# A fused attention and two-stage expert kernel: partial sums of the first stage added by GpSimd's transfers, with other priorities

## The chip, the cores and the metric

The program runs on one core of one Trainium2 chip. The metric is the device time of one execution in microseconds. Three executions of the kernel before gave 853.74, 858.54 and 864.12 us, so the time before is their median, 858.54 us.

## The reference

Three layers follow each other on 2304 tokens of width 512 (4 batches x 576 tokens, 8 heads of 64):

```python
# attention in a causal window of 64 keys
scores = where(0 <= rel < 64, q @ k.T / 8, -1e9);  x = softmax(scores) @ v
# first moe stage: dense, d_ff 2048; w_in and w_out are float64
h = x @ w_in;  g = h - tanh(h);  x = g @ w_out
# second moe stage: top 1 of 8 experts, d_ff 1024
logits = (x / |x|) @ (emb / |emb|).T / tau
e = argmax(logits);  gate = softmax(logits)[e]
out = gate * (relu(x @ w1[e]) @ w2[e])
```

## The kernel before

Tokens are cut into 9 chunks `c` of 256. The program has two parts. In the first, up to some 561 us of the profiled execution, come the attention (`t_attn`, 18 units `n`, two per chunk, four heads each), the decoding of the float64 weights (`t_decode`, 32 halves), the first moe stage (`t_moe1`, 72 steps) and the routing of each finished chunk (`t_route`). In the second the experts follow one after another. The change lies in the first part.

**A step.** `t_moe1` takes two blocks of 128 of the d_ff columns for one chunk. TensorE makes `h` (`mm1`, 24 matmuls of 128x256 on the lines of `mm3`), ScalarE and VectorE make `g - tanh` and split it in a high and a low part `gh` (VectorE lines L639, L648, L652, L656, L666), and TensorE multiplies by `w_out` into two PSUM accumulators `o` (`mm2`, 12 matmuls of 128x512).

**Segments.** While weights are still being decoded, chunks 0 to 3 are worked on in four segments of two steps each, so that every decoded block serves four chunks at once. The list `order` says which segment comes when; chunks 4 to 8 then run their eight steps in one segment. At a segment's end `t_sum` takes the sums out of PSUM. The first segment of a chunk is copied to a buffer of the pool `st` (4 buffers of 128x1024) and stored to `partd[c]` in DRAM. Each later one first loads `partd[c]` to an `st` buffer, VectorE adds the two accumulators to it (L698), and it is stored again, except after the last segment: there the sum `x2` goes on to `t_route`. That stores it, takes its squares on ScalarE (L726), a power on GpSimd (L735), transposes it on TensorE (L751), makes logits and slots, and scatters 8-byte entries of a list with GpSimd (L848, two scatters per chunk, each waiting for the one before).

The `st` buffers also hold raw weights, chunks of `x` on their way from DRAM, and the transposed `x2` of the routing.

**The order of the work.** Nothing is ordered by hand. Every function calls `SC.add` with the engines that can do a task, a duration for each, what it reads, writes and allocates, and a priority. `Sched.run` then plays the program in its own time and gives an idle engine the ready task of the lowest priority; an engine's queue afterwards runs in exactly that order. So a changed priority or duration reorders every engine. A GpSimd transfer is planned with 1.04 for its issue and `lat` on top, and a hand-over between engines with `OTHER = 0.21`. The priorities come from `slot_t` (TC per block while weights are decoded, TM after that), `TA` (how far apart attention units are), `AHEAD` and `WLEAD`:

```python
T0, TC, TM = 8, 3.7, 2.9
TA = 14
AHEAD, LEAD, WLEAD = 10, 12.0, 6.0
```

Of the kernel before, what the change touches and what calls it, by code (L numbers as in the profile page):

```python
# [16 lines left out]
ALU = mybir.AluOpType  # L17
# [144 lines left out]
def attn_moe_moe2(ctx, tc, q, k, v, w_in, w_out, emb, tau, w1, w2, out):  # L162
# [58 lines left out]
    def copies(o, i, act, dve):  # L221
        return {ACT: (act, lambda: nc.scalar.copy(out=o(), in_=i())), DVE: (dve, lambda: nc.vector.tensor_copy(out=o(), in_=i()))}  # L222
# [116 lines left out]
    def t_decode(f, o, w, pr):  # L339
        raw, tmp = Buf("st"), Buf("tmp")  # L340

        def load():
            r = raw.t.bitcast(U32)
            if o == 0:
                nc.sync.dma_start(
                    out=r.rearrange("p (k f) -> p k f", k=KD),
                    in_=w_in.bitcast(U32)[:, f * 256:(f + 1) * 256].rearrange("(k p) f -> p k f", p=P),
                )
            else:
                nc.sync.dma_start(out=r, in_=w_out.bitcast(U32)[f * P:(f + 1) * P, :])  # L350

        def words(i):
            return raw.t.bitcast(U32).rearrange("p (n w) -> p n w", w=2)[:, :, i]

        hi = lambda: w.t[:, o * 512:o * 512 + 512]
        lo = lambda: w.t[:, 1024 + o * 512:1536 + o * 512]
        ti = lambda: tmp.t.bitcast(U32)
        tf = lambda: words(1).bitcast(F32)

        def d1():  # L360
            nc.scalar.activation(out=tmp.t, in_=words(1).bitcast(F32), func=AF.Abs)

        def d2():
            nc.vector.tensor_scalar(out=tmp.t, in0=tmp.t, scalar1=float(2.0 ** -15), scalar2=None, op0=ALU.max)

        def d3():
            nc.vector.tensor_scalar(
                out=ti(), in0=ti(), scalar1=3, scalar2=0x3FFFFFF8,
                op0=ALU.logical_shift_left, op1=ALU.bitwise_and,
            )  # L370

        def d4():
            nc.vector.scalar_tensor_tensor(
                out=ti(), in0=words(0), scalar=29, in1=ti(), op0=ALU.logical_shift_right, op1=ALU.bitwise_or
            )

        def d5():
            nc.vector.scalar_tensor_tensor(
                out=words(1), in0=words(1), scalar=0xC0000000, in1=ti(), op0=ALU.bitwise_and, op1=ALU.bitwise_or
            )  # L380

        SC.add({DMA: (1.5, load)}, writes=[(raw, 0)], allocs=[raw], prio=pr - 6.0)
        SC.add(
            {ACT: (0.52, d1)}, reads=[(raw, 0)], writes=[(tmp, 0)], allocs=[tmp] + ([w] if o == 0 else []), prio=pr
        )
        SC.add({DVE: (0.335, d2)}, writes=[(tmp, 0)], prio=pr)
        SC.add({DVE: (0.335, d3)}, writes=[(tmp, 0)], prio=pr)
        SC.add({DVE: (0.6, d4)}, reads=[(raw, 0)], writes=[(tmp, 0)], prio=pr)
        SC.add({DVE: (0.6, d5)}, reads=[(tmp, 0)], writes=[(raw, 0)], prio=pr)
        SC.add({ACT: copies(hi, tf, 0.52, 0.335)[ACT]}, reads=[(raw, 0)], writes=[(w, o)], prio=pr)  # L390

        def sub(eng):
            return lambda: eng.tensor_tensor(out=lo(), in0=tf(), in1=hi().bitcast(F32), op=ALU.subtract)  # L393

        SC.add({DVE: (0.6, sub(nc.vector))}, reads=[(raw, 0), (w, o)], writes=[(w, 2 + o)], prio=pr)
# [7 lines left out]
    def t_attn(n, pr, direct, spill):  # L403
# [52 lines left out]
        def s_mm():  # L456
# [7 lines left out]
                        )  # L464

        SC.add(
            {PE: (1.1, s_mm)}, reads=lq, writes=[(as_[0], 0), (as_[1], 0)], allocs=[*as_, pr_], prio=pr + 1.5
        )
        st = {}

        def mx(hh):
            if hh == 0:
                st["m"] = small("mx", [P, 2 * NB], bufs=3)
            for i in range(NB):
                first = [(c * NB + 2 * (i % 2) + d) % (S // BLK) == 0 for d in range(2)]
                m_ = 1 + hh if first[0] else 2 - hh if first[1] else 0
                nc.vector.tensor_tensor_reduce(
                    out=pr_.t[:, hh * NB + i, :], in0=as_[hh].t[:, i * P:(i + 1) * P], in1=mask[m_],
                    scale=-SCALE, scalar=3.0e38, op0=ALU.add, op1=ALU.min, accum_out=st["m"][:, hh * NB + i:hh * NB + i + 1],
                )  # L480

        def ex(hh):
            if hh == 0:
                st["den"] = small("den", [P, 2 * NB], bufs=3)
            for i in range(hh * NB, (hh + 1) * NB):
                nc.scalar.activation(  # L486
                    out=pr_.t[:, i, :], in_=pr_.t[:, i, :], func=AF.Exp, bias=st["m"][:, i:i + 1], scale=-1.0,
                    accum_out=st["den"][:, i:i + 1],
                )
# [20 lines left out]
                nc.tensor.transpose(out=ap[hh].t[:, i * P:(i + 1) * P], in_=pr_.t[:, hh * NB + i, :], identity=ident)  # L510

        for hh in range(2):
            SC.add({DVE: (0.9, lambda hh=hh: mx(hh))}, reads=[(as_[hh], 0)], writes=[(pr_, hh)], prio=pr + 1.5)
        for hh in range(2):
            SC.add({ACT: (1.54, lambda hh=hh: ex(hh))}, writes=[(pr_, hh)], prio=pr + 1.5)
        SC.add({DVE: (0.29, dn)}, writes=[(pr_, 0), (pr_, 1)], prio=pr + 1.5)
        for hh in range(2):
            SC.add(
                {DVE: (0.6, lambda hh=hh: nm(hh)), ACT: (1.2, lambda hh=hh: nm_act(hh))}, writes=[(pr_, hh)], prio=pr + 1.5
            )  # L520
            SC.add(
                {PE: (0.43, lambda hh=hh: tp(hh))}, reads=[(pr_, hh)], writes=[(ap[hh], 0)], allocs=[ap[hh], pT[hh]],
                prio=pr + 3,
            )
            SC.add(
                copies(lambda hh=hh: pT[hh].t, lambda hh=hh: ap[hh].t, 0.48, 0.6), reads=[(ap[hh], 0)],
                writes=[(pT[hh], 0)], prio=pr + 3,
            )
# [75 lines left out]
    def t_moe1(c, f, acc, first, last, pr):  # L604
# [74 lines left out]
        for j in range(2):  # L679
            SC.add(  # L680
                {PE: (1.39, lambda j=j: mm2(j))}, reads=[(wt[f + j], 1), (wt[f + j], 3), (gs, 0), (gs, 1)],
                writes=[(acc[0], 0), (acc[1], 0), ("mm2", c, f + j)], prio=pr + 3.0,
            )


    def t_sum(c, acc, more, last, near, pr):

        x2 = Buf("st")
        if more:
            SC.add(  # L690
                {DMA: (1.5, lambda: nc.sync.dma_start(out=x2.t, in_=partd[c]))},
                reads=[("part", c), ("mm2", c, near)], writes=[(x2, 0), (x2, 1)], allocs=[x2], prio=pr - 12.0,
            )
        for i in range(2):
            h = slice(i * DM, (i + 1) * DM)
            alts = copies(lambda h=h: x2.t[:, h], lambda i=i: acc[i].t, 0.48, 0.6)
            if more:
                alts = {DVE: (0.6, lambda i=i, h=h: nc.vector.tensor_tensor(  # L698
                    out=x2.t[:, h], in0=acc[i].t, in1=x2.t[:, h], op=ALU.add))}
            SC.add(alts, reads=[(acc[i], 0)], writes=[(x2, i)], allocs=[x2] if i == 0 and not more else [], prio=pr)  # L700
        if not last:
            SC.add(
                {DMA: (1.5, lambda: nc.sync.dma_start(out=partd[c], in_=x2.t))},
                reads=[(x2, 0), (x2, 1)], writes=[("part", c)], prio=pr + 2.0,
            )
        return x2
# [518 lines left out]
    setup2()  # L1225
    t_setup()
    SC.free[POOL] = 5.5
    T0, TC, TM = 8, 3.7, 2.9
    TA = 14

    def slot_t(s):
        return T0 + TC * min(s, KF) + TM * max(s - KF, 0)
# [3 lines left out]
    order += [(1, 4, 8, ""), (0, 4, 8, ""), (0, 8, 12, ""), (1, 8, 12, ""), (3, 8, 12, "load"), (2, 8, 12, "load")]  # L1236
    order += [(2, 12, KF, ""), (3, 12, KF, ""), (1, 12, KF, "load"), (0, 12, KF, "load")]
    order += [(c, 0, KF, "load") for c in range(4, NC)]
    AHEAD, LEAD, WLEAD = 10, 12.0, 6.0
    start, due, s_ = {}, {}, 0  # L1240
    for c, f0, f1, how in order:
        start[c, f0] = s_
        for f in range(f0, f1):
            due.setdefault(f, slot_t(s_ + f - f0))
        s_ += f1 - f0
    t_weights(lambda f, o: due[f] - WLEAD + 3.0 * o)
    for n in range(NC * NU):
        c = n // NU
        first = [x[3] for x in order if x[0] == c]
        t_attn(  # L1250
            n, min(TA * n, slot_t(start[c, 0]) - AHEAD + 5.0 * (n % NU)) if c else 1.0 * n,
            first[0] if first[0] != "load" else None, "load" in first,
        )
    for c, f0, f1, how in order:
        if how == "load":
            t_xload(c, slot_t(start[c, f0]) - LEAD)
        acc = [Buf("o") for _ in range(2)]
        s_ = start[c, f0]
        for f in range(f0, f1, 2):
            t_moe1(c, f, acc, f0, f1 - 1, slot_t(s_ + f - f0))  # L1260
        end = slot_t(s_ + f1 - f0)
        x2 = t_sum(c, acc, f0 > 0, f1 == KF, f1 - 5 if f1 - 5 > f0 else f0, end - 12.0 if c + 1 < NC else 0.0)
        if f1 == KF:
            t_route(c, x2, end if c + 1 < NC else 0.0)
        if c == NC - 2:
            t_turns(end)
            t_list(0, 0, end)
# [180 lines left out]
```

## Time and profile before

| | |
|---|---|
| time, median of three | 858.54 us (853.74 to 864.12) |
| the profiled execution | 861.28 us, span 859.5 us |
| mean granted TensorE clock | 0.971 |
| TensorE busy | 788.2 us, 92% of the span |
| VectorE busy | 604.9 us, 70% |
| ScalarE busy | 483.3 us, 56% |
| GpSimd busy | 89.8 us, 10% |
| DMA | 111.39 MB, of it 13.13 MB on GpSimd's queue |

The shares are means over two parts with different limits. In the slices of the page VectorE stands at 9 tenths up to about 300 us and at 6 or 7 after that, while TensorE is at 7 to 9 in the first third and at 9 behind it. Busy time of TensorE counts a matmul to its modelled end, which reaches over the next one's start, so the distance between starts is the better price of a matmul; the same holds for VectorE's short latencies.

### The profile page before, as it was taken

To read this page: it belongs to the slowest core of one execution; us is meant where nothing else is said; L and a number is where in the kernel's file an instruction comes from. 1 tells how busy PE (TensorE), PEld (TensorE's weight loads), DVE (VectorE), ACT (ScalarE), POOL (GpSimd) and SP (SyncE) were. 2 spreads that over 40 slices of the span, in tenths; PEclk is the share of its full clock that TensorE was granted. 3 is DMA by queue.
4 is the path that set the end of the run, shared out by engine and by line. 5 is a ranking of instruction groups with operands and counts; after the bars stand their busy time and mean duration, and the time that the engine had idled before them with its cause. 6 is when DMAs were issued, how large, how long until landed. Compare 5 with 4: busy or idle time off the path is not lost. (4 is left out here: it accounts for less than half of the span.)

```text
span 859.5 us, 15577 instructions
## 1 busy us (share of the span) xinstructions
PE 788.2 (92%) x5703; PEld 687.3 (80%) x5703; DVE 604.9 (70%) x1498; ACT 483.3 (56%) x1121; POOL 89.8 (10%) x116
## 2 busy tenths in 40 slices
PE   4788799999899899999899999896999998997995
PEld 4577687988798789898788988775889887886984
DVE  6999999999999677767557678972177377244720
ACT  5799788867695658555555566731244343233421
POOL 2000000000002110010101001012022122121210
PEclk9899999999999999999999999997999999998998
DMA  9765754657654621100100004535067376235511
GB/s 288 239 205 153 240 175 151 201 176 239 204 168 88 155 73 38 62 1 1 50 1 25 1 26 144 183 116 171 13 195 239 108 241 225 75 100 174 161 40 37
DMA packets 67436, 111.39 MB, mean 130 GB/s; under 512 B 8580, under 2 KB 44420, under 8 KB 67344
## 3 DMA queue, kind: packets, MB, share of 16 engines
q1 hardware_dynamic: 62448, 97.07, 35.7%
q0 software_dynamic: 4896, 13.13, 4.9%
q8 instruction: 53, 0.87, 0.5%
q14 instruction: 39, 0.32, 0.1%
HBM read 89.57 MB, written 21.66 MB: 129 GB/s over the span
## 5 line engine op out<-in xcount | busy, mean ns | idle before, releaser
L600 PE MATMUL h<-x,w 128*128 128x256 f32 x712 | 206.6, 290 | 10.0 <-DVE g L652 9.4
L601 PE MATMUL h<-x,w 128*128 128x256 f32 x712 | 203.5, 286 | 2.0 <-DVE x L576 1.9
L602 PE MATMUL h<-x,w 128*128 128x256 f32 x712 | 203.0, 285 | 0.3 <-DVE w L393 0.2
L600 PE MATMUL o<-w,gh 128*128 128x512 f32 x464 | 188.7, 407 | 6.3 <-ACT gh L662 5.9
L602 PE MATMUL o<-w,gh 128*128 128x512 f32 x464 | 184.9, 399 | 3.6 <-DVE gh L666 2.2
L601 PE MATMUL o<-w,gh 128*128 128x512 f32 x464 | 184.0, 397 | 0.0
L600 PEld LDWEIGHTS h<-x,w 128*128 128x128 f32 x712 | 137.8, 194 | 17.6 <-issue 9.7
L601 PEld LDWEIGHTS h<-x,w 128*128 128x128 f32 x712 | 138.0, 194 | 6.1 <-DVE x L576 2.7
L602 PEld LDWEIGHTS h<-x,w 128*128 128x128 f32 x712 | 137.8, 194 | 0.8 <-DVE w L393 0.8
L602 PEld LDWEIGHTS o<-w,gh 128*128 128x128 f32 x464 | 88.4, 190 | 29.8 <-DVE gh L666 6.4
L600 PEld LDWEIGHTS o<-w,gh 128*128 128x128 f32 x464 | 88.6, 191 | 25.4 <-ACT gh L662 6.6
L601 PEld LDWEIGHTS o<-w,gh 128*128 128x128 f32 x464 | 88.9, 192 | 14.1
L222 ACT CAST w<-st 128x512 fp32r<-128x512 f32 x116 | 70.2, 629 | 33.1 <-DMA st<-in_moe_w_dram 21.4
L866 DVE TENSOR_TENSOR w<-st,w 128x512 fp32r<-128x512 f32 x128 | 82.8, 686 | 4.3 <-ACT w L222 3.3
L639 DVE SCALAR_TENSOR_TENSOR g<-g 128x512 f32<-128x512 f32 x72 | 49.5, 688 | 30.6 <-ACT g L631 30.4
L644 ACT ACTIVATE g<-h 128x512 f32<-128x512 f32 x72 | 42.9, 596 | 38.2 <-DVE g L648 31.6
L627 ACT ACTIVATE g<-h 128x512 f32<-128x512 f32 x72 | 42.6, 594 | 36.9 <-PE h L602 31.6
L662 ACT CAST gh<-g 128x512 fp32r<-128x512 f32 x72 | 44.1, 616 | 33.6 <-DVE g L656 29.4
L652 DVE TENSOR_TENSOR g<-h,g 128x512 f32<-128x512 f32 x72 | 49.4, 687 | 17.4 <-ACT g L644 16.2
L978 ACT ACTIVATE gh<-h 128x256 fp32r<-128x256 f32 x50 | 19.1, 383 | 73.3 <-PE h L602 54.8
L648 DVE TENSOR_TENSOR g<-h,g 128x512 f32<-128x512 f32 x72 | 49.6, 689 | 8.8 <-ACT g L644 5.2
L486 ACT ACTIVATE pr<-pr,mx 128x128 f32<-128x128 f32 x144 | 55.7, 391 | 0.1
(179 smaller groups left out, 1292.4 us busy)
## 6 DMA issues: line engine op xcount, KB each, us to landing
st<-in_moe_w_dram SPq DMA_DIRECT2D x64, 512.0 KB, 5.3
st<-in_moe_w_in_dram SPq DMA_DIRECT2D x16, 512.0 KB, 4.3
st<-in_moe_w_out_dram SPq DMA_DIRECT2D x16, 512.0 KB, 4.7
v<-in_v_dram SPq DMA_DIRECT2D x16, 512.0 KB, 3.7
part<-st SPq DMA_DIRECT2D x12, 512.0 KB, 2.7
st<-part SPq DMA_DIRECT2D x12, 512.0 KB, 9.6
k<-in_k_dram SPq DMA_DIRECT2D x16, 320.0 KB, 5.3
q<-in_q_dram SPq DMA_DIRECT2D x18, 256.0 KB, 3.0
```

The source lines that it names most:

```text
L222: return {ACT: (act, lambda: nc.scalar.copy(out=o(), in_=i())), DVE: (dve, lambda: nc.vector.tensor_copy(out=o(), in_=i()))}
L486: nc.scalar.activation(out=pr_.t[:, i, :], in_=pr_.t[:, i, :], func=AF.Exp, bias=st["m"][:, i:i + 1], scale=-1.0, accum_out=st["den"][:, i ...
L600: nc.tensor.matmul(out=ps, lhsT=ah, rhs=bh, start=start, stop=False)
L601: nc.tensor.matmul(out=ps, lhsT=ah, rhs=bl, start=False, stop=False)
L602: nc.tensor.matmul(out=ps, lhsT=al, rhs=bh, start=False, stop=stop)
L627: {ACT: (0.48, lambda: nc.scalar.activation(out=u(), in_=hp.t, func=AF.Square))},
L639: {DVE: (0.6, lambda: nc.vector.scalar_tensor_tensor(out=sq(), in0=sq(), scalar=SQ_B, in1=u(), op0=ALU.add, op1=ALU.mult))},
L644: {ACT: (0.48, lambda: nc.scalar.activation(out=u(), in_=hp.t, func=AF.Tanh))},
L648: {DVE: (0.6, lambda: nc.vector.tensor_tensor(out=sq(), in0=hp.t, in1=sq(), op=ALU.mult))},
L652: {DVE: (0.6, lambda: nc.vector.tensor_tensor(out=u(), in0=hp.t, in1=u(), op=ALU.subtract))},
L662: {ACT: (0.52, lambda: nc.scalar.copy(out=gh(), in_=sq()))}, reads=[(g, 1), (acc[0], "-"), (acc[1], "-")],
L866: return lambda: eng.tensor_tensor(out=w.t[:, b], in0=raw.t[:, a], in1=w.t[:, a].bitcast(F32), op=ALU.subtract)
```

## The change

`t_sum` no longer loads the partial sum. Every segment's accumulators are copied to an `st` buffer, by ScalarE or VectorE, whichever the scheduler finds free. The first segment is stored as before. A middle segment is added to `partd[c]` in DRAM by a transfer that GpSimd issues. The last segment's copy is the destination of such a transfer: `partd[c]` is added to the rows of `x2` in SBUF, and everything in `t_route` waits for that. Both are planned with `lat=3.0`. The priorities of weight loads, score matmuls, attention units, `mm2` and `t_sum` change too.

```diff
-        SC.add({DMA: (1.5, load)}, writes=[(raw, 0)], allocs=[raw], prio=pr - 6.0)
+        SC.add({DMA: (1.5, load)}, writes=[(raw, 0)], allocs=[raw], prio=pr - 8)
...
-                writes=[(acc[0], 0), (acc[1], 0), ("mm2", c, f + j)], prio=pr + 3.0,
+                writes=[(acc[0], 0), (acc[1], 0), ("mm2", c, f + j)], prio=pr + 2,
...
-        if more:
-            SC.add(
-                {DMA: (1.5, lambda: nc.sync.dma_start(out=x2.t, in_=partd[c]))},
-                reads=[("part", c), ("mm2", c, near)], writes=[(x2, 0), (x2, 1)], allocs=[x2], prio=pr - 12.0,
-            )
         for i in range(2):
             h = slice(i * DM, (i + 1) * DM)
-            alts = copies(lambda h=h: x2.t[:, h], lambda i=i: acc[i].t, 0.48, 0.6)
-            if more:
-                alts = {DVE: (0.6, lambda i=i, h=h: nc.vector.tensor_tensor(
-                    out=x2.t[:, h], in0=acc[i].t, in1=x2.t[:, h], op=ALU.add))}
-            SC.add(alts, reads=[(acc[i], 0)], writes=[(x2, i)], allocs=[x2] if i == 0 and not more else [], prio=pr)
-        if not last:
+            SC.add(
+                copies(lambda h=h: x2.t[:, h], lambda i=i: acc[i].t, 0.48, 0.6), reads=[(acc[i], 0)], writes=[(x2, i)],
+                allocs=[x2] if i == 0 else [], prio=pr,
+            )
+        if last and not more:
+            return x2
+        if last:
+            SC.add(
+                {POOL: (1.04, lambda: nc.gpsimd.dma_start(out=x2.t, in_=partd[c], accum_op=ALU.add))},
+                reads=[("part", c)], writes=[(x2, 0), (x2, 1)], prio=pr + 1.0, lat=3.0,
+            )
+        elif more:
+            SC.add(
+                {POOL: (1.04, lambda: nc.gpsimd.dma_start(out=partd[c], in_=x2.t, accum_op=ALU.add))},
+                reads=[(x2, 0), (x2, 1)], writes=[("part", c)], prio=pr + 2.0, lat=3.0,
+            )
+        else:
...
-    T0, TC, TM = 8, 3.7, 2.9
-    TA = 14
+    T0, TC, TM = 8, 4.3, 2.9
+    TA = 20
...
-    AHEAD, LEAD, WLEAD = 10, 12.0, 6.0
+    AHEAD, LEAD, WLEAD = 12, 12.0, 4
...
-    t_weights(lambda f, o: due[f] - WLEAD + 3.0 * o)
+    t_weights(lambda f, o: due[f] - WLEAD + 4 * o)
...
-            n, min(TA * n, slot_t(start[c, 0]) - AHEAD + 5.0 * (n % NU)) if c else 1.0 * n,
+            n, min(TA * n, slot_t(start[c, 0]) - AHEAD + 2 * (n % NU)) if c else 1 * n,
...
-        x2 = t_sum(c, acc, f0 > 0, f1 == KF, f1 - 5 if f1 - 5 > f0 else f0, end - 12.0 if c + 1 < NC else 0.0)
+        x2 = t_sum(c, acc, f0 > 0, f1 == KF, end - 8 if c + 1 < NC else 0.0)
```

Left out are the five places in `t_attn` where `pr + 1.5` becomes `pr + 1`.

GpSimd's queue in the kernel before, from the power of the setup on: per routed chunk one power and two scatters, and nothing else.

```order
L295 TENSOR_TENSOR enrm<-enrm,half 8x1
L735 TENSOR_TENSOR nrm<-ss,half 128x2
L848 DMA lst<-pg,su 18432x2 x2
L735 TENSOR_TENSOR nrm<-ss,half 128x2
L848 DMA lst<-pg,su 18432x2 x2
```

The same queue in the changed kernel, from the last two adds into DRAM (L704) on; the destinations of L699 are the rows `x2` of chunks 2, 3, 1 and 0, in this order, and lines behind `t_sum` have moved by six.

```order
L704 DMA part_77<-st_2730 128x1024
L704 DMA part_76<-st_2824 128x1024
L699 DMA st_2981<-part_76 128x1024
L741 TENSOR_TENSOR nrm<-ss,half 128x2
L699 DMA st_3095<-part_77 128x1024
L854 DMA lst<-pg,su 18432x2
L741 TENSOR_TENSOR nrm<-ss,half 128x2
L854 DMA lst<-pg,su 18432x2 x2
L699 DMA st_3320<-part_75 128x1024
L854 DMA lst<-pg,su 18432x2
L741 TENSOR_TENSOR nrm<-ss,half 128x2
L854 DMA lst<-pg,su 18432x2
L699 DMA st_3511<-part_74 128x1024
```

The adding transfers of chunks 1 and 0 now stand behind scatters of the chunks before them, which wait for each other.

TensorE's queue in the changed kernel at the first of the four routings: the transposes of chunk 2's `x2` (`st_2981`) stand in the midst of a step's `mm2`.

```order
L601 MATMUL o_3001<-w_2248,gh_2999 128x512
L602 MATMUL o_3001<-w_2248,gh_2999 128x512
L757 MATMUL a_3053<-ident,st_2981 128x128 x4
L757 MATMUL a_3060<-ident,st_2981 128x128 x4
L600 MATMUL o_3000<-w_2438,gh_3025 128x512
L601 MATMUL o_3000<-w_2438,gh_3025 128x512
```

Between the last matmul into that chunk's accumulators and these transposes there are now 36 `mm1` and 12 `mm2` matmuls of other chunks; in the kernel before there were 24 `mm1` matmuls.

ScalarE's queue in the changed kernel at the same place: the squares of `st_2981` (L732) stand ahead of the tanh (L644) of a step.

```order
L631 ACTIVATE g_3021<-g_3021,sqa 128x512
L635 ACTIVATE big_3022<-g_3021,nu_98 128x512
L732 ACTIVATE tmp_3045,ss<-st_2981 128x512
L644 ACTIVATE g_3021<-h_2968 128x512
L732 ACTIVATE tmp_3045,ss<-st_2981 128x512
```

The first square now waits for the adding transfer, with the step's tanh queued behind it.

## Rows read from the trace of the kernel before

**Rows 1.** The page: busy time of each engine, share of the span, instructions.

```profile
PE 788.2 (92%) x5703; PEld 687.3 (80%) x5703; DVE 604.9 (70%) x1498; ACT 483.3 (56%) x1121; POOL 89.8 (10%) x116
```

**Rows 2.** Busy us by stretch: PE, PEld, DVE, ACT, POOL; clock, DMA share, GB/s.

```profile
44.60:175.60 131.00, 119.08 (x1071) 103.38 (x1071) 126.44 (x325) 112.61 (x290) 0.60 (x1) 0.99 0.60 189
175.60:208.80 33.20, 31.19 (x273) 27.84 (x272) 32.87 (x73) 22.21 (x45) 0.00 (x0) 1.00 0.63 205
208.80:321.70 112.90, 107.48 (x918) 93.04 (x917) 96.05 (x279) 79.58 (x206) 12.05 (x12) 0.97 0.51 144
321.70:439.60 117.90, 115.22 (x826) 103.19 (x826) 82.04 (x183) 70.34 (x146) 6.42 (x6) 1.00 0.09 28
439.60:561.30 121.70, 115.71 (x741) 102.80 (x739) 89.94 (x180) 74.02 (x132) 7.81 (x8) 0.99 0.22 73
```

**Rows 3.** The same stretches, instructions on `o` alone: first figure is TensorE.

```profile
44.60:175.60 131.00, 46.16 (x180) 33.80 (x180) 7.19 (x11) 1.74 (x3) 0.99 0.60 189
175.60:208.80 33.20, 14.47 (x60) 11.00 (x60) 3.85 (x6) 0.00 (x0) 1.00 0.63 205
208.80:321.70 112.90, 42.26 (x168) 30.33 (x168) 7.68 (x12) 0.00 (x0) 0.97 0.51 144
```

**Rows 4.** Waits of TensorE, first 560 us: total, times, longest.

```profile
PE h L600 <- DVE g L652: 10.7, 10, 2.8
...
PE o L600 <- ACT gh L662: 5.9, 3, 3.0
```

**Rows 5.** Timeline of TensorE: start, us, instruction.

```profile
161.06 0.28 PE L602 MATMUL h<-x,w 128*128 128x256 f32 x1
161.18 0.28 PE L600 MATMUL h<-x,w 128*128 128x256 f32 x1
...
167.57 0.40 PE L602 MATMUL o<-w,gh 128*128 128x512 f32 x1
167.80 0.39 PE L600 MATMUL o<-w,gh 128*128 128x512 f32 x1
...
221.18 1.10 PE L461 MATMUL a<-k,q 64*64 64x128 f32 x32
...
262.19 1.04 PE L510 MATMUL a<-ident,pr 128*128 128x128 f32 x8
```

**Rows 6.** Timeline of VectorE: start, us, instruction.

```profile
246.14 0.28 DVE L477 CUSTOM_DVE_ANT_0 pr<-a,mask 128x128 f32<-128x128 f32 x1
...
246.35 0.28 DVE L477 CUSTOM_DVE_ANT_0 pr<-a,mask 128x128 f32<-128x128 f32 x1
...
249.05 1.28 DVE L698 TENSOR_TENSOR st<-o,st 128x512 f32<-128x512 f32 x2
250.25 0.68 DVE L648 TENSOR_TENSOR g<-h,g 128x512 f32<-128x512 f32 x1
...
251.44 0.41 DVE L222 CAST x<-st 128x512 fp32r<-128x512 f32 x1
251.78 0.75 DVE L656 COPY_PREDICATED g<-big,g 128x512 f32<-128x512 uint16 x1
...
261.23 0.15 DVE L833 TENSOR_TENSOR sl<-a,oh 128x16 f32<-128x16 f32 x1
```

**Rows 7.** Transfers: count, KB each, median us from issue to landing.

```profile
part<-st SPq DMA_DIRECT2D x12, 512.0 KB, 2.7
st<-part SPq DMA_DIRECT2D x12, 512.0 KB, 9.6
...
lst<-pg,su POOLq DMA_INDIRECT x18, 4.0
...
g<-x2d,gi POOLq DMA_INDIRECT x16, 5.9
```

**Rows 8.** Timeline of GpSimd: a chunk's two scatters.

```profile
262.10 1.61 POOL L848 DMA_INDIRECT lst<-pg,su  x1 [8.42 <-DVE cum L843]
266.75 1.10 POOL L848 DMA_INDIRECT lst<-pg,su  x1 [3.04 <-DMA lst<-pg,su]
```

More of the change, by code (lines that the diff above doesn't have):

```diff
@@ L466, in t_attn @@
         SC.add(
-            {PE: (1.1, s_mm)}, reads=lq, writes=[(as_[0], 0), (as_[1], 0)], allocs=[*as_, pr_], prio=pr + 1.5
+            {PE: (1.1, s_mm)}, reads=lq, writes=[(as_[0], 0), (as_[1], 0)], allocs=[*as_, pr_], prio=pr + 1
         )
@@ L512, in t_attn @@
         for hh in range(2):
-            SC.add({DVE: (0.9, lambda hh=hh: mx(hh))}, reads=[(as_[hh], 0)], writes=[(pr_, hh)], prio=pr + 1.5)
+            SC.add({DVE: (0.9, lambda hh=hh: mx(hh))}, reads=[(as_[hh], 0)], writes=[(pr_, hh)], prio=pr + 1)
         for hh in range(2):
-            SC.add({ACT: (1.54, lambda hh=hh: ex(hh))}, writes=[(pr_, hh)], prio=pr + 1.5)
-        SC.add({DVE: (0.29, dn)}, writes=[(pr_, 0), (pr_, 1)], prio=pr + 1.5)
+            SC.add({ACT: (1.54, lambda hh=hh: ex(hh))}, writes=[(pr_, hh)], prio=pr + 1)
+        SC.add({DVE: (0.29, dn)}, writes=[(pr_, 0), (pr_, 1)], prio=pr + 1)
         for hh in range(2):
             SC.add(
-                {DVE: (0.6, lambda hh=hh: nm(hh)), ACT: (1.2, lambda hh=hh: nm_act(hh))}, writes=[(pr_, hh)], prio=pr + 1.5
+                {DVE: (0.6, lambda hh=hh: nm(hh)), ACT: (1.2, lambda hh=hh: nm_act(hh))}, writes=[(pr_, hh)], prio=pr + 1
             )
@@ L681, in t_moe1, with t_sum @@
                 {PE: (1.39, lambda j=j: mm2(j))}, reads=[(wt[f + j], 1), (wt[f + j], 3), (gs, 0), (gs, 1)],
-                writes=[(acc[0], 0), (acc[1], 0), ("mm2", c, f + j)], prio=pr + 3.0,
+                writes=[(acc[0], 0), (acc[1], 0), ("mm2", c, f + j)], prio=pr + 2,
             )
-    def t_sum(c, acc, more, last, near, pr):
+    def t_sum(c, acc, more, last, pr):
         x2 = Buf("st")
-        if more:
-            SC.add(
-                {DMA: (1.5, lambda: nc.sync.dma_start(out=x2.t, in_=partd[c]))},
-                reads=[("part", c), ("mm2", c, near)], writes=[(x2, 0), (x2, 1)], allocs=[x2], prio=pr - 12.0,
-            )
         for i in range(2):
             h = slice(i * DM, (i + 1) * DM)
-            alts = copies(lambda h=h: x2.t[:, h], lambda i=i: acc[i].t, 0.48, 0.6)
-            if more:
-                alts = {DVE: (0.6, lambda i=i, h=h: nc.vector.tensor_tensor(
-                    out=x2.t[:, h], in0=acc[i].t, in1=x2.t[:, h], op=ALU.add))}
-            SC.add(alts, reads=[(acc[i], 0)], writes=[(x2, i)], allocs=[x2] if i == 0 and not more else [], prio=pr)
-        if not last:
+            SC.add(
[15 more added lines that the diff above has]
+        else:
             SC.add(
```

## The prediction

> **What bounds the kernel now.** I read the busy times of the page first, then the same busy times cut into stretches, and then who makes TensorE wait. TensorE is busy for 788.2 of the span's 859.5 us, so all that any change can win is the rest and what hides between the starts of its matmuls [rows 1]. The profiled execution took 861.28 us, 1.8 more than its span and 2.7 more than the median of 858.54; I sum differences and take them from the median.
>
> The stretches are cut at the ends of steps 1, 16, 21, 35, 53 and 72 of the first moe stage [rows 2]; the 180, 60 and 168 matmuls into `o` (12 per step) are 15, 5 and 14 steps [rows 3]. In the first VectorE is busy for 126.4 of 131.0 us, in the second for 32.9 of 33.2: there it sets the pace. In the third it has 96.1 of 112.9, in the fourth 82.0 of 117.9. What TensorE needs is counted from starts: 0.12 us for a 128x256 matmul, 0.23 for a 128x512, 0.13 for a transpose (1.04 for 8), 0.034 for a score matmul and, taken alike, one of P times V [rows 5]. With the counts of the program's order this is 96.7 us of work in the third stretch (86% of it) and 112.0 in the fourth (95%). So up to step 21 VectorE bounds, from there to 35 neither quite, and after that TensorE. TensorE's waits say the same: the longest are for VectorE's L652, the last read of `h` (10.7 us), and for ScalarE's `gh` (5.9) [rows 4].
>
> **What the order takes off and moves.** The adds are 24, 0.60 us each by the distance of starts (two from 249.05 to 250.25 [rows 6]), 14.4 us of VectorE. In their place come 24 copies; of all copies of accumulators VectorE now has 19 where it had 9, ScalarE 23 where it had 9. With the moved attention units, VectorE's change by stretch is, each count by 0.60, by 0.34 for the fast one-input operations and by 0.21 for a masked minimum [rows 6]:
> - steps 2 to 16: 6 adds out (-3.6), 2 copies of accumulators in (+1.2), other copies +1.2, decoding instructions moved behind step 16 (-3.7), attention (-3.0), the rest -0.6; sum -8.5.
> - steps 17 to 21: 6 adds out (-3.6), 3 copies in (+1.8), the decoding that was moved here (+5.6), an attention unit's minima (+1.7), parts of steps (+3.6); sum about +9.4.
> - steps 22 to 35: 12 adds out (-7.2), 5 copies in (+3.0), 28 masked minima (-5.9), 5 normalisations (-3.0) and the small rest of three attention units, decoding (-2.8), splits and other copies (-3.6), a step's parts; sum about -22.9.
> - steps 36 to 53: attention moved here, +6.9; steps 54 to 72: +4.1.
>
> TensorE's work changes little: in the third stretch 12 fewer `mm1`, 24 transposes, 32 score and 48 P-times-V matmuls, -1.4 - 3.1 - 1.1 - 1.6 = -7.2, to 89.5; in the fourth +2.1, in the fifth +3.0.
>
> **The gain by stretch.** Where VectorE bounds, the length goes with its work. First: 131.0 x 117.9 / 126.4 = 122.2, 8.8 less. Second: 33.2 x 42.3 / 32.9 = 42.7, 9.5 more. In the third VectorE's work falls to 73.2, TensorE's 89.5 is now the larger, and I give it the fill that TensorE has in the fourth, where VectorE is as light: 89.5 / 0.95 = 94.2, 18.7 less. The fourth becomes 114.1 / 0.95 = 120.1, 2.2 more, and the fifth 3.2 more (121.7 by 116 to 113 us of work). The sum is 12.6 us less. The low end: the third keeps its 86% (104.1, 8.8 less), sum 2.7. The high end: VectorE doesn't bound the second, TensorE's 35.2 us there fill 95% (37.1, 3.9 more), sum 18.2. I take 12.6, since the fourth stretch, with its light VectorE, is the nearest to what the third becomes.
>
> **What the adding transfers cost.** No transfer of this kind is in the trace. The eight into DRAM have no reader for some ten steps or more, and GpSimd did almost nothing there (0.60 and 0.00 us in the first two stretches [rows 2]); they cost nothing on the path, except that each holds one of four `st` buffers until it lands. If that cover goes, a weight load on SP's queue waits with all loads behind it; against it 12 loads of the partial sum are gone, which held a buffer for 9.6 us each before the add [rows 7].
>
> The four that end chunks 2, 3, 1 and 0 are on the path: TensorE's transposes, ScalarE's squares and with them the next step's tanh wait for the landing. Let L be the time from issue to landing. The cover is TensorE's work that the order puts ahead of each chunk's transposes, and it is short:
> - chunk 2: 36 x 0.12 + 12 x 0.23 = 7.08 us after the last accumulating matmul. In this time: two copies on VectorE (1.20), two hand-overs (0.21 each, the scheduler's figure), L. Stall L - 5.46.
> - chunk 3: 5.56 of work, one copy on each engine (0.60). Stall L - 4.54.
> - chunk 1: its transfer stands on GpSimd behind both scatters of chunk 2 and the first of chunk 3. A scatter waits 0.87 from VectorE's L833 [rows 6, 8], its follower starts 4.65 after it, and an issue takes 1.10 [rows 8]: 0.87 + 4.65 + 4.65 + 1.10 = 11.27 from chunk 2's slots to this issue. TensorE has 15.3 between. Stall L - 4.03.
> - chunk 0: behind the first scatter of chunk 1: 0.87 + 1.10 + L against 6.74. Stall L - 4.77.
>
> Together 4L - 18.8 where all are above zero. For L the trace gives bounds: 2.7 us for a plain transfer of 512 KB from SP and 4.0 for the tiny scatter from GpSimd, 5.9 for GpSimd's gathers of 256 KB, 9.6 for SP's loads of 512 KB in traffic [rows 7]. Landing at 4.0 or below costs nothing. I take 5.9: a GpSimd issue, and the gather's bytes are the nearest. Stall 0.44 + 1.36 + 1.87 + 1.13 = 4.8; at 9.6 it is 19.6. Against the trace stands a formula of the Trainium skill, page "DMA: Bandwidth & Descriptors", section "Anatomy of one DMA": some 2.0 us fixed plus the bytes at 436 GB/s. For 512 KB that is an estimate of 3.2 us, by which the stall would be nothing and the time 846; the scatter's 4.0 for a kilobyte already disagrees with it.
>
> **Forecast.** 858.5 - 12.6 + 4.8 = 850.7 us.
>
> **Rivals.**
> - *Early landing.* L is 4.0 or less, the stalls vanish, and the gain stands whole: 858.5 - 12.6 = 845.9; with the high end 840.3. For it: GpSimd and the DMA engines (0.51 busy in the third stretch [rows 2]) have room, and the scheduler plans 1.04 + 3.0. Against it: even the kilobyte scatter needs 4.0 [rows 7]. Chance 0.20.
> - *Late landing, slower than before.* The add has to read two operands, and if L is 9.6, TensorE, ScalarE and VectorE stand still together at four places: 858.5 - 12.6 + 19.6 = 865.5. It decides from L = 7.9 on, where 4L - 18.8 passes 12.6; each further microsecond costs 4. For it: SP's loads did take 9.6, and scatters queue behind each other [rows 7, 8]. Against it: those loads waited behind others on their queue. The Trainium skill, page "SBUF — State Buffer", in the box on VectorE blocking DMAs under "SBUF: two separate sides", says that GpSimd can't write its descriptors while VectorE runs a fast two-port copy, which speaks for this rival. The trace agrees as far as one scatter's issue took 1.61 and the next 1.10 [rows 8]; 0.51 longer at each of four issues would be 2.0 us, an estimate. Chance 0.15.
> - *The freed VectorE time buys nothing.* The third stretch keeps its 86%, because TensorE waits there for chains of dependent instructions in a fixed order and not for a full engine (VectorE has 17 us free in it already [rows 2]), and the moved attention brings its own waits later: 858.5 - 2.7 + 4.8 = 860.6. Against it: the longest waits are for VectorE's L652 [rows 4]. Chance 0.25.
>
> **How the numbers follow.** The forecast has 0.40, and as its own range 846 to 856. A measurement of this kernel can tell about 1% (8.6 us) from no change. Faster by more than that, below 850.0: the early case 0.20 and just under half of the forecast, 0.40. Slower by more, above 867.1: more than half of the late case (L above 10.0, or the low gain with it) and a fifth of the third rival, 0.14. The rest, 0.46, is within 1%. For 8 in 10 the range runs from 842, inside the early case, to 866, which takes in L = 9.6 with the middle gain.
>
> **What would show it right or wrong.** In the profile after: steps 2 to 16 some 9 us shorter, with VectorE still above 95%; steps 22 to 35 near 94 us plus the stalls; TensorE's waits at the transposes of four chunks, a wait that didn't stand among the long ones, with 0.4 to 2 us each; GpSimd's adds of 512 KB landing 5 to 7 us after issue. No wait at the transposes would speak for the early case, waits of 4 us or more for the late one. The forecast is wrong if the reordered start (step 1 is unchanged in the sum, but the order of decoding and attention is not) brings waits for loads that the sums can't see, or if the adds into DRAM hold `st` buffers so long that weight loads come late.

## The result, and the profile after

The changed kernel takes 865.02 us (median of 20, 858.59 to 871.98), the kernel before 857.51 in the same rounds (851.95 to 864.12). The ratio is 1.0073 [1.0048, 1.0098]: slower by 0.7%, where 850.7 and a gain of 0.9% were forecast. It is worked out from the single executions without the one in the slower state (871.98), and so differs from the quotient of the medians, 1.0088. The profiled execution took 864.76 us, its span is 862.9. Against before's 859.5 that is 3.4 us of the medians' 7.5, since before's profiled execution (861.28) lies above its median; the traces are compared as they stand.

Busy time on the page of the changed kernel (to [rows 1]):

```profile
PE 785.4 (91%) x5703; PEld 685.0 (79%) x5703; DVE 593.5 (69%) x1478; ACT 496.0 (57%) x1153; POOL 101.6 (12%) x128
```

VectorE lost 11.4 us, where my counts by stretch add up to 11.0, and ScalarE took on 12.7. By stretch the counts are further off (-6.1, +6.8, -18.9, +3.2, +4.6 by these rows and [rows 2], where -8.5, +9.4, -22.9, +6.9, +4.1 were counted), so the sum agrees by luck. No share says why that didn't pay. The stretches do, cut at the same steps as [rows 2], same columns, of the changed kernel:

```profile
42.40:167.90 125.50, 114.26 (x983) 98.87 (x982) 120.37 (x304) 103.17 (x259) 3.44 (x4) 0.99 0.55 163
167.90:209.90 42.00, 38.61 (x321) 33.65 (x320) 39.70 (x87) 33.61 (x74) 2.56 (x3) 1.00 0.69 184
209.90:319.40 109.50, 96.33 (x695) 83.12 (x694) 77.18 (x212) 69.82 (x161) 17.73 (x18) 0.97 0.43 96
319.40:440.90 121.50, 120.88 (x1036) 107.21 (x1036) 85.21 (x235) 85.45 (x210) 6.40 (x6) 1.00 0.20 61
440.90:565.20 124.30, 119.25 (x793) 106.20 (x791) 94.51 (x188) 78.56 (x148) 8.18 (x8) 0.99 0.24 80
```

In the third row TensorE is busy for 96.3 of 109.5 us and VectorE for 77.2: neither bounds, 13 us are empty on TensorE. In the fourth TensorE is full. The lengths of the stretches, each taken from the start of the last matmul into `o` of its last step, in us:

| steps | before | predicted change | after | change | error |
|---|---|---|---|---|---|
| up to 1 | 43.9 | not in the sum | 41.7 | -2.2 | -2.2 |
| 2 to 16 | 130.7 | -8.8 | 125.4 | -5.3 | +3.5 |
| 17 to 21 | 33.4 | +9.5 | 42.0 | +8.6 | -0.9 |
| 22 to 35 | 112.2 | -18.7 + 4.8 | 109.6 | -2.6 | +11.3 |
| 36 to 53 | 118.4 | +2.2 | 121.4 | +3.0 | +0.8 |
| 54 to 72 | 122.4 | +3.2 | 124.3 | +1.9 | -1.3 |

Behind step 72 the kernels take 298.6 us before and 298.4 after. So the miss of 11.2 us in these traces lies in steps 22 to 35, where the four adding transfers end a chunk; the other errors cancel. (Between the forecast's 7.8 us less and the medians' 7.5 more are 15.3; the other 4 come from where the two profiled executions lie among their like.) A difference of 1 or 2 us in a row says little: six runs of the experiments below have this kernel's order up to step 21, and there step 1 ends at 41.5 to 43.9 and steps 2 to 16 take 125.4 to 127.0.

What TensorE waits for in the first 560 us (to [rows 4]):

```profile
PE a L757 <- DMA st<-part: 10.9, 4, 4.9
PE h L600 <- DVE g L652: 7.8, 10, 3.0
PE a L461 <- DMA k<-in_k_dram: 7.3, 2, 4.6
PE o L602 <- DVE gh L666: 5.0, 7, 1.1
```

The transposes (L757) lead this list now; they weren't among the long waits before. The view of the transfer's line, L699, says who else stood and how long the transfers took; below it the same of L704, the adds into DRAM:

```profile
who waited for it (us, times):
  ACT tmp L732: 13.0, 4
  PE a L757: 10.9, 4
...
DMA to landing us min/median/max: 5.5/7.0/9.7
```

```profile
L704 POOL DMA_DIRECT2D part<-st x8: 854/856/1132, 135.8 to 226.0; - x8
...
who waited for it (us, times):
busy tenths in 40 slices 0000000000000000000000000000000000000000
DMA to landing us min/median/max: 5.3/5.4/5.7
```

Nobody waits for the eight adds into DRAM. The four that end chunks differ among themselves, and the timeline of GpSimd (start, us, instruction, idle time before it) shows by what:

```profile
239.21 0.87 POOL L699 DMA_DIRECT2D st<-part  x1 [12.39 <-ACT x L222]
...
250.50 0.91 POOL L699 DMA_DIRECT2D st<-part  x1 [2.67 <-DVE tmp L222]
...
266.61 0.95 POOL L854 DMA_INDIRECT lst<-pg,su  x1 [4.47 <-DVE cum L849]
267.57 1.00 POOL L699 DMA_DIRECT2D st<-part  x1
273.82 1.00 POOL L854 DMA_INDIRECT lst<-pg,su  x1 [5.26 <-DMA lst<-pg,su]
...
288.36 1.03 POOL L854 DMA_INDIRECT lst<-pg,su  x1 [8.38 <-DVE cum L849]
289.39 1.00 POOL L699 DMA_DIRECT2D st<-part  x1
```

Chunks 2 and 3 have a transfer by itself. Those of chunks 1 and 0 are issued in the moment in which a scatter's issue ends, with no idle time between. What moved in 267 to 269 (queue: packets, MB, share of the DMA engines) and what was issued then (count, KB, us to landing), and the same for 289 to 290.3; `q1` is SP's queue, `q0` GpSimd's:

```profile
q1 hardware_dynamic: 316, 0.32, 61.7%
...
st<-part POOLq DMA_DIRECT2D x1, 512.0 KB, 9.7
xTd<-tmp SPq DMA_DIRECT2D x1, 256.0 KB, 10.3
...
q0 software_dynamic: 30, 0.00, 1.9%
...
st<-part POOLq DMA_DIRECT2D x1, 512.0 KB, 8.5
```

The other two landed after 5.5. Chunk 1's transfer has a second neighbour: in the 6 us after its issue SP's queue moved 0.70 MB, a load of `v` and the store to `xTd`. Beside the transfers of the other three chunks SP's queue moved nothing. TensorE's timeline at chunk 1, and its stretches before, at and after these transposes (columns as in [rows 2]):

```profile
277.32 1.97 PE L757 MATMUL a<-ident,st 128*128 128x128 f32 x8 [4.89 <-DMA st<-part]
278.94 0.77 PE L600 MATMUL o<-w,gh 128*128 128x512 f32 x1
279.51 0.63 PE L601 MATMUL o<-w,gh 128*128 128x512 f32 x1
```

```profile
272.00:277.30 5.30, 0.43 (x2) 0.01 (x1) 0.52 (x1) 0.00 (x0) 1.00 (x1) 0.97 0.46 89
277.30:281.00 3.70, 3.68 (x14) 3.15 (x14) 2.30 (x5) 2.84 (x7) 0.72 (x1) 0.58 0.38 142
281.00:285.00 4.00, 4.00 (x30) 3.18 (x29) 1.31 (x6) 1.60 (x4) 0.00 (x0) 1.00 0.00 0
...
298.00:302.00 4.00, 3.97 (x16) 3.32 (x18) 1.58 (x4) 2.41 (x6) 0.72 (x1) 0.64 0.35 131
```

In the first of these TensorE, VectorE and ScalarE nearly stand still together (0.43, 0.52 and 0.00 us of 5.3). In the second TensorE runs at a granted clock of 0.58, a mean of its levels of 2.4 and 1.2 GHz after it had stood for 4.9 us: eight transposes take 1.97 us where they took 1.07 at chunk 3. The last row is the same at chunk 0, after a wait of 4.2. The price beside the waits is 0.42 x 3.7 + 0.36 x 4.0 = 3.0 us.

### The profile page after: what moved, and what is told of

Read it like the earlier page. It is cut to its first block, busy times and chain, and to the rows that moved or that the text cites. A ratio compares the mean times of both kernels' runs of the same rounds, so it can differ in the third digit from the quotient of the medians.

```text
span 862.9 us, 15608 instructions
## 1 busy us (share of the span) xinstructions
PE 785.4 (91%) x5703; PEld 685.0 (79%) x5703; DVE 593.5 (69%) x1478; ACT 496.0 (57%) x1153; POOL 101.6 (12%) x128
## 5 line engine op out<-in xcount | busy, mean ns | idle before, releaser
L602 PEld LDWEIGHTS o<-w,gh 128*128 128x128 f32 x464 | 87.9, 189 | 31.6 <-DVE gh L666 10.4
L222 ACT CAST w<-st 128x512 fp32r<-128x512 f32 x116 | 70.0, 630 | 22.9 <-DMA st<-in_moe_w_dram 19.1
L639 DVE SCALAR_TENSOR_TENSOR g<-g 128x512 f32<-128x512 f32 x72 | 49.4, 686 | 29.8 <-ACT g L631 29.7
L644 ACT ACTIVATE g<-h 128x512 f32<-128x512 f32 x72 | 42.9, 595 | 36.3 <-DVE g L648 28.0
L648 DVE TENSOR_TENSOR g<-h,g 128x512 f32<-128x512 f32 x72 | 49.6, 688 | 10.4 <-ACT g L644 7.3
```

The source lines that it names most:

```text
L602: nc.tensor.matmul(out=ps, lhsT=al, rhs=bh, start=False, stop=stop)
L639: {DVE: (0.6, lambda: nc.vector.scalar_tensor_tensor(out=sq(), in0=sq(), scalar=SQ_B, in1=u(), op0=ALU.add, op1=ALU.mult))},
L644: {ACT: (0.48, lambda: nc.scalar.activation(out=u(), in_=hp.t, func=AF.Tanh))},
L648: {DVE: (0.6, lambda: nc.vector.tensor_tensor(out=sq(), in0=hp.t, in1=sq(), op=ALU.mult))},
```

## The experiments

Each was timed against the kernel before on its own chip, so ratios are compared. The theory after the result: the four transfers are the loss, above all the two behind scatters. Its rival: the moved attention and decoding, that is the priorities, cost the time.

**Priorities alone**: the changed kernel with the old `t_sum`, its loads and VectorE adds; the priority at which `t_sum` itself is called goes back with it.

```
...
-        x2 = t_sum(c, acc, f0 > 0, f1 == KF, end - 8 if c + 1 < NC else 0.0)
+        x2 = t_sum(c, acc, f0 > 0, f1 == KF, f1 - 5 if f1 - 5 > f0 else f0, end - 12.0 if c + 1 < NC else 0.0)
```

> All the changed priorities, but partial sums loaded by SP and added by VectorE as in the kernel before (24 adds, no adding transfer). Theory A: no landing on the path, VectorE as busy as before; steps 2 to 16 some 4 us shorter than in the kernel before, the rest equal, time 853 to 859. Rival E, the priorities themselves cost (attention moved behind step 35 and loads bunched): time 862 or more without any adding transfer.

851.76 us, ratio 0.9954 [0.9921, 0.9987]; step 72 ends at 552.7 us, 8.3 before the kernel before. The priorities gain; the rival falls.

**The old last add in the changed kernel**: the middle segments still add in DRAM by GpSimd, the last one loads by SP and adds by VectorE.

```
...
+                {DMA: (1.5, lambda: nc.sync.dma_start(out=x2.t, in_=partd[c]))},
...
+            if load:
+                alts = {DVE: (0.6, lambda i=i, h=h: nc.vector.tensor_tensor(
+                    out=x2.t[:, h], in0=acc[i].t, in1=x2.t[:, h], op=ALU.add))}
...
-                {POOL: (1.04, lambda: nc.gpsimd.dma_start(out=x2.t, in_=partd[c], accum_op=ALU.add))},
...
```

> The middle segments are still added in DRAM by GpSimd's transfers, with the changed priorities; only the last segment is handled as in the kernel before: SP loads the partial sum ahead of time and VectorE adds (8 adds). Theory A (the four landings on the path cost it): no wait at the transposes, steps 22 to 35 in about 98 us, time 853 to 856, under the kernel before. Rival C: 863 to 867. Rival D, the eight adds into DRAM cost by holding the st buffers: time stays above the kernel before (857.5) although the transposes don't wait.

851.32 us, ratio 0.995 [0.9918, 0.9981], step 72 ends at 552.0. Sixteen VectorE adds fewer, against priorities alone, can't be told from nothing; the loss lies in the four last transfers.

**A later plan for the same transfers**: one number, the landing time that the scheduler reckons for them.

```
-                reads=[("part", c)], writes=[(x2, 0), (x2, 1)], prio=pr + 1.0, lat=3.0,
+                reads=[("part", c)], writes=[(x2, 0), (x2, 1)], prio=pr + 1.0, lat=6.5,
```

> Only the planned duration of the four adding transfers into the last rows changes, from 1.04 + 3.0 to 1.04 + 6.5, so the transposes and squares are queued later. Theory A (the late landing, which the order does not cover, costs the 10.9 us of waits): waits fall to 3 us or less and the time to about 856. Rival C (the waits don't set the time): waits fall, time stays at 863 to 867. If the later routing brings new waits elsewhere, the stretch of steps 22 to 35 stays above 105 us although the waits at the transposes are gone.

848.33 us, ratio 0.9894 [0.9856, 0.9931], faster than both kernels; no wait for the transfers is left, and step 72 ends at 553.3. The expected 856 had the waits alone in it. The transfers land at 5.2 to 6.8, since the new plan also moved them on GpSimd; the timeline there, and the landing of the transfer shown:

```profile
264.84 1.08 POOL L854 DMA_INDIRECT lst<-pg,su  x1 [3.54 <-DMA lst<-pg,su]
...
267.54 0.97 POOL L699 DMA_DIRECT2D st<-part  x1 [1.62 <-issue]
```

```profile
st<-part POOLq DMA_DIRECT2D x1, 512.0 KB, 6.8
```

With 1.62 us behind the scatter it is chunk 1's transfer again, 2.9 us sooner. That isn't the distance alone: SP's queue moved nothing beside it here.

**The add taken out of the transfer**: the four last ones overwrite, in the changed kernel's own order.

```
-                {POOL: (1.04, lambda: nc.gpsimd.dma_start(out=x2.t, in_=partd[c], accum_op=ALU.add))},
+                {POOL: (1.04, lambda: nc.gpsimd.dma_start(out=x2.t, in_=partd[c]))},
```

> The four last transfers of a chunk are issued by GpSimd as before, in the very same order on every engine, but overwrite the rows instead of adding to them (the earlier segments' copy of the last segment is lost, so the last segment's own sum is left out). Theory A, the add makes the landing long: landing falls from 7.0 us (5.5 to 9.7) to about 4.5, TensorE's waits at the transposes from 10.9 to under 4 us, time about 858. Rival B, the landing is long because of GpSimd's queue, the distance and the traffic, whatever is moved: landing stays at 6 us or more, waits at 8 or more, time 862 to 866. Rival C, the waits don't set the time, what TensorE waits here it would wait elsewhere: waits fall, time stays within 2 us of 865.

869.93 us, ratio 1.0145 [1.0104, 1.0186]. The total says nothing here: the other values route the tokens differently, and the second part holds more work (308.1 us behind step 72 and not 298.4). In steps 22 to 35 the transposes wait 6.2 us in two places in place of 10.9 in four. The two transfers by themselves land at 3.8 and 3.7, with no wait; those behind scatters at 9.0 and 6.3. So theory A holds for the first two and rival B for the others: the add costs some 1.8 us of landing (5.5 against 3.7), and the place of chunks 1 and 0 costs a plain transfer about as much (5.3 and 2.6 us) as an adding one (4.2 and 3.0). Chunk 1's again has SP's traffic beside it (0.61 MB in 6 us), chunk 0's has none.

**The scatter ahead taken away**: the same order, where the first scatters of chunks 3 and 1 are small copies on GpSimd. This leaves 256 tokens out of the experts' lists, so only the first part compares.

```
...
+                if i == 0 and c in (1, 3):
+                    nc.gpsimd.tensor_copy(out=small("scr", [P, 2], U32), in_=st["su"])
+                    return
```

> The changed kernel with its order on every engine, but the first scatter of chunk 3 and that of chunk 1, which stand right ahead of the adding transfers of chunks 1 and 0 on GpSimd, are small copies on GpSimd (128 tokens each of these chunks are left out of the list, and so of the output). Theory F, the transfer's data wait behind the scatter's in GpSimd's queue: these two land in 5.5 to 6 us as the two others do, instead of 9.7 and 8.6; the waits at the transposes fall from 10.9 to about 4, step 72 ends 6 to 9 us earlier, time 856 to 859. Rival G, other traffic at that moment (loads on SP's queue) makes them late: they still need 8 us or more, time 863 to 866.

858.25 us, ratio 0.9975 [0.9948, 1.0001], 0.98% below the changed kernel's; step 72 ends at 558.4, 6.1 us sooner, by two scatters of a kilobyte. The wait of TensorE:

```profile
PE a L757 <- DMA st<-part: 4.8, 4, 2.4
```

Chunk 1's transposes start 7.7 us after the issue in place of 9.7, chunk 0's 6.1 in place of 8.6. So a scatter directly ahead costs 2.0 and 2.5 us. Chunk 0 is left 0.6 above the 5.5 of a lone transfer, chunk 1 2.2. In this run a scatter is issued 1.25 us behind each, and SP's queue moves 0.60 MB in the 6 us beside chunk 1's and nothing beside chunk 0's. In lat50 below, chunk 1's transfer has a scatter issued 1.6 us behind it and no traffic of SP, and lands at 5.4. That points to SP's traffic for the 2.2, but it wasn't tried by itself, and elsewhere such traffic cost little (0.47 MB beside chunk 2's transfer in the run at 3.0 with the old priorities, whose reader starts after 5.4).

**The other half, the old priorities with the new `t_sum`**, at planned landings of 3.0 and 6.5: the kernel before with the changed kernel's `t_sum`.

```
...
-        x2 = t_sum(c, acc, f0 > 0, f1 == KF, f1 - 5 if f1 - 5 > f0 else f0, end - 12.0 if c + 1 < NC else 0.0)
+        x2 = t_sum(c, acc, f0 > 0, f1 == KF, end - 8 if c + 1 < NC else 0.0)
```

> The priorities of the kernel before with the changed handling of the sums (copies, eight adds into DRAM, four into the last rows, planned with 1.04 + 3.0). Theory A, the uncovered landings cost wherever the priorities put them: two of the transfers stand right behind a scatter or close to one, waits of 6 to 11 us at the transposes, time 858 to 864, not faster than the kernel before. Rival H, only the changed priorities bring the landings on the path: waits under 3 us, time at or below 855, since VectorE has 24 adds less.

> As the run before, with the four transfers into the last rows planned with 1.04 + 6.5. Theory A: few waits at the transposes, and what is left is the worth of 24 adds taken off VectorE under the old priorities: 852 to 857. If taking them off is worth nothing (last_load and prio_only differ by 16 adds and by half a microsecond), the time is that of the kernel before, 856 to 859.

879.25 us, ratio 1.0201 [1.0173, 1.0228], and 867.11 us, 1.0057 [1.0033, 1.0082]. The planned landing is worth 1.4% here too (8.0 us of waits at the transposes against 0.6). But both lose elsewhere, which I had not expected: steps 2 to 16 last 159.6 and 162.1 us where they lasted 130.7. The stretch of the second (columns as in [rows 2]), and TensorE's longest wait of the first part (11.9 us of it in this stretch, where the kernel before has 2.9):

```profile
43.20:205.20 162.00, 138.57 (x1318) 118.50 (x1319) 155.14 (x425) 137.58 (x374) 3.59 (x4) 0.93 0.62 189
```

```profile
PE o L600 <- ACT gh L662: 14.9, 5, 7.2
```

VectorE has 425 instructions there and not 325 [rows 2], ScalarE 374 and not 290: decoding and attention units that stood behind step 16 now stand ahead of it, and `gh` is queued behind them. The granted clock of the stretch is 0.93 where it was 0.99. Step 35 still ends 10 us later than before. The scheduler packed the freed VectorE time with early work; that this is what hurts under the old priorities is read from the order, and which of the altered priorities prevents it was not tried.

**Scatters planned later as well**: lat65, and 3.2 in place of 2.0 for a scatter.

```
-            SC.add({POOL: (1.04, sc)}, reads=[("su", c), ("pg", c)], writes=[("lst", 0)], prio=pr, lat=2.0)
+            SC.add({POOL: (1.04, sc)}, reads=[("su", c), ("pg", c)], writes=[("lst", 0)], prio=pr, lat=3.2)
```

> lat65 with the scatters planned with 1.04 + 3.2 in place of 1.04 + 2.0, near their measured 4.0 to 4.7. If the plan's other errors on GpSimd's queue still cost, 844 to 847; if not, 847 to 850 as lat65.

860.12 us, ratio 0.9996 [0.9975, 1.0016], outside both expectations. Up to step 53 it is lat65's equal (427.4); then a gather that was pushed back 7 us holds TensorE, and step 72 ends 5.2 us later than in lat65. Its wait in 480 to 560 us, and GpSimd's timeline:

```profile
PE a L941 <- DMA v<-x2d,gi: 8.3, 2, 6.4
```

```profile
529.46 1.99 POOL L918 DMA_INDIRECT v<-x2d,gi  x1 [15.82 <-DVE g L639]
531.75 6.88 POOL L918 DMA_INDIRECT v<-x2d,gi  x1 [0.30 <-issue]
```

One number of the plan, altered for scatters, moved a gather some 270 us behind the first of them, and more than half of the 8.6 us between the two profiled executions was given back there; the other 3.4 lie behind step 72 and weren't followed up.

**How much distance**: planned landings of 5.0 and 9.5, by lat65's line with `lat=5.0` and `lat=9.5`.

> The changed kernel with one number of its planner altered: the landing time that it reckons for the four last adding transfers, 5.0 us in place of 3.0 (6.5 in lat65). Theory (each microsecond that TensorE waits at a chunk's transposes is one microsecond of the kernel, and without such waits the new priorities end step 72 at 552 to 554 us): the transfers still land 5.5 us after issue, one right behind a scatter at 7 to 10; TensorE waits 0 to 5 us in all at the transposes, step 72 ends at 553 plus this wait, ratio 0.990 to 0.997. Rival (such a stall stops all engines and costs more than its wait, as the 19 us lost in steps 22 to 35 for 10.9 us of waits suggest): with 3 us of wait step 72 ends 5 to 6 us later than in lat65.

> As lat50, with 9.5 us planned, the longest landing that was seen. Theory: no wait for the transfers, step 72 ends at 552 to 554 us and the ratio is that of lat65 (0.986 to 0.993), since once the transfer is covered more distance buys nothing. Rival (more distance lets ScalarE's squares and the routing slip too, so that the chains behind the transposes end later): steps 22 to 35 get 3 us or more longer than lat65's 90.4 and the ratio is above 0.993.

849.05 us, ratio 0.991 [0.9878, 0.9942], and 848.39, 0.9896 [0.9846, 0.9947]; waits at the transposes 0.2 and none, step 72 at 551.5 and 552.0. Anything from 5.0 to 9.5 serves; lat95's steps 22 to 35 take 90.7, so more distance costs nothing either, and its rival falls.

The run at 5.0 has a further use: its steps 22 to 35 hold the same 695 records of matmuls as the changed kernel and as no_scatter, with waits taken away. In this order the stretches of lat50, no_scatter and no_add:

```profile
211.40:306.70 95.30, 92.92 (x695) 81.01 (x694) 79.75 (x216) 67.84 (x151) 17.24 (x18) 1.00 0.48 110
```

```profile
211.10:313.30 102.20, 95.16 (x695) 81.70 (x694) 77.38 (x212) 69.80 (x161) 15.94 (x18) 0.98 0.43 102
```

```profile
210.00:314.50 104.50, 96.01 (x696) 82.46 (x695) 77.62 (x212) 69.97 (x161) 16.01 (x18) 0.97 0.39 100
```

From 95.3 without waits, the changed kernel's 10.9 of waits and 3.0 of clock make 109.2 (measured 109.5). no_scatter's 4.8 and 1.7 (clock 0.57 for 4.0 us after chunk 1) make 101.8 (102.2); no_add's 6.2 and 3.0 (0.50 for 6.0 us after chunk 1) make 104.5 (104.5). A wait costs itself, and those of 2.4 to 4.9 us at chunks 1 and 0 cost 1.4 to 3.0 us of clock on top. Of the two expectations for lat50 the first came true; the second had no wait to be tried on, but these sums bear it out in that the waits aren't all.

## Why the prediction was wrong

**The step that failed** is "I take 5.9": one landing time L for all four adding transfers. It measured 5.5, 5.5, 9.7 and 8.5, so the term 4.8 was 10.9. For the lone transfers the value was near: 5.9 taken, 5.5 measured. For chunks 1 and 0 I had worked out when GpSimd gets to the transfer behind the scatters, and priced the queue as waiting ahead of the issue alone; the transfer still landed late after its issue. That a scatter just ahead does this is shown by no_scatter, where it is taken away (and the next scatter moves up behind the transfer) and the readers start 2.0 and 2.5 us sooner. Of the 7.2 us by which the two landed later than 5.5 that is 4.5; of the rest 2.2 stand at chunk 1, beside 0.70 MB on SP's queue, and were not tried by themselves. How scatter and transfer get into each other's way isn't settled. Directly behind a scatter and without traffic of SP one landed at 7.1 (lat95) and one at 8.5 (here), so the price of the place was between 1.6 and 3.0 us; lat95's chunk 0, 2.4 us behind one, still took 6.9.

**The formulas around it held.** With the measured landings they give 5.5 - 5.46 = 0.04, 5.5 - 4.54 = 0.96, 9.7 - 4.03 = 5.67 and 8.5 - 4.77 = 3.73, together 10.4. Measured: 0.30, 1.53, 4.89, 4.16, together 10.9. The cover that I counted from the order was right to a microsecond at each place; L alone was not.

**A term was missing**: TensorE's clock after such a wait, 3.0 us. It is missing from the 94.2 us of the sum and not a cost that the kernel before is free of: there the same stretch has a clock of 0.97 too [rows 2].

**The late rival** has this place and this mechanism, and two of the four waits passed the 4 us that were to speak for it. That the measured 865.02 is all but its 865.5 is luck: it has waits of 19.6 us where 10.9 were measured, no term for the clock, and a gain of 12.6 us that didn't come.

**The gains by stretch.** The third stretch, which I had given TensorE's fill of the fourth, was to take 94.2 us without stalls, and lat50 shows 95.3, so the third rival's 104.1 falls. That the freed VectorE time bought this is not shown. With priorities alone the same stretch is (columns as in [rows 2]):

```profile
205.60:306.40 100.80, 97.51 (x768) 84.46 (x766) 93.51 (x259) 73.86 (x183) 13.42 (x12) 1.00 0.44 137
```

There VectorE still has all adds and is busy for 93.5 us, TensorE is as full (97.5 of 100.8 against 92.9 of 95.3 in lat50), and it holds 768 matmuls in place of 695. Steps 17 to 21 and 36 to 72 came within 1.3 us. Steps 2 to 16 gained 5.3 in place of 8.8: VectorE was busy for 120.4 of 125.5 us, 96% as asked for, but with 120.4 us of work where I had counted 117.9. Step 1, left out, gained 2.2, which is what executions of one order differ by. In the recorded sum the items of steps 17 to 21 add up to 9.1 and not to 9.4, which is 0.3 us of the forecast. So of the error of 11.2 us at step 72, 6.1 are the landings, 3.0 the clock, and the rest, 2.1, is what is left of small errors of both signs. Without waits at the transposes step 72 ends 7.6 to 9.5 us ahead of the kernel before's 561.0, where the sum had 12.6.

**What the gain is due to.** That it would come from adds taken off VectorE was my reading of the sum; priorities alone reach step 72 at 552.7, and the runs with all 24 adds off and no waits at 551.5 to 553.3. In total those are at 0.989 to 0.991 and the two with VectorE's last adds at 0.995, with intervals that overlap: whether the adding transfers bring half a per cent of their own stays open.

**The formula**: the Trainium skill, page "DMA: Bandwidth & Descriptors", section "Anatomy of one DMA", has one that gave an estimate of 3.2 us for 512 KB. A plain transfer from GpSimd by itself landed at 3.7 to 3.8 in no_add, so it is near for that; with the add 5.2 to 5.8, once 6.4 (lat50), and behind a scatter up to 9.7, which the formula doesn't hold. The longer issue that I had worked into the late rival isn't there: the four issues took 0.87 to 1.00. Nor did the row that I took for agreement show it: in the 1.61 us of that scatter's issue VectorE ran no copy, but L639 and two of the adds (L698).

## What to carry to other kernels

When work moves from an engine to an asynchronous transfer, the cover must be counted for each transfer with its neighbours on the queue, since a small scatter just ahead added 1.6 to 3.0 us to a landing of 5.5, and the worst landing, 9.7, had another queue's traffic beside it as well. Where a scheduler plans with a landing time, a number that is too small is paid in full at every reader, and one that is too large cost nothing here: 5.0, 6.5 and 9.5 gave the same time, 3.0 lost 1.8%. Try such a number before taking the transfer back, and look at the whole program afterwards, since the same edit at another operation moved a gather and gave 1% back.

## What was not expected of the hardware

- A scatter of 128 small rows delays a transfer of 512 KB that is issued right behind it on GpSimd, adding or not: 8.5 against 5.5 with the add, 6.3 against 3.7 to 3.8 without, where SP's queue moved nothing; 9.7 and 9.0 where it moved 0.6 to 0.7 MB beside it.
- The add in a transfer into SBUF costs 1.8 us of landing and about 0.3 of issue (0.58 to 0.61 us without it, 0.86 to 1.01 with it). Adding into DRAM landed at 5.3 to 5.7, as adding into SBUF by itself; no plain transfer from GpSimd into DRAM was run beside it.
- After waits of 4.9 and 4.2 us TensorE was granted 0.58 and 0.64 over the next 4 us, and 1.00 again after that; after 2.4 us in no_scatter 0.57, after 4.3 us in no_add 0.50 for 6.0 us. After the wait of 1.5 us at chunk 3 eight transposes took 1.07, as they do without a wait (1.03 to 1.07 in lat65).
- The issues of two gathers on GpSimd, 1.00 and 0.96 us in lat65, took 1.99 and 6.88 in lat65_scat, where they came 7 and 8 us later; what held them wasn't tried.
